# Two key tiles, then two value tiles: reordering the loads of a decode attention kernel group by group

## The chip, the core and the metric

The kernel runs on one core of a Trainium2 chip. The metric is the device time of one execution in microseconds (us), median of the runs shown. All tiles are float32.

## What is computed

The program adds three things for a batch of two rows: the input `x`, a sliding-window attention over a key and a value cache, and a gated feed-forward layer. Both branches take the same normalised `x`.

```python
xn = _layernorm(x)                                   # x: [2, 1, 512]
q = xn @ wq                                          # 32 heads of 128
k = k_cache[:, :, Sk - W:, :]                        # 8 kv heads, W = 4096 rows of 128, each kv head for 4 q heads
v = v_cache[:, :, Sk - W:, :]
p = softmax(q . k * 128 ** -0.5)
A = (p . v) @ wo                                     # wo: [4096, 512]
gate, up = xn @ W_gate, xn @ W_up                    # [512, 1792] each
h = gate * (gate > 0) * up
B = h @ W_down                                       # [1792, 512]
return x + A + B
```

## The kernel before

**Loads.** Everything large comes through one ring of four buffers of 4 MB (tag `ring`, pool at L62), on SyncE's queue (`load`, L71 to L74): 23 loads in the order in which the code calls them. A load waits, on that queue and in order, until the buffer of the load four places ahead of it has been used up. The order is: wq in two tiles (L122), `wg` and `wu` (L226, L227), then in the loop at L395 one tile of keys and one tile of values in turn, then `wd` (L413) and `wo` in two tiles, the second in four pieces (L449 to L452). `x` comes on ScalarE's queue in five pieces (L119 to L121); the tile `x2` is read by the layer norm (L188, L203) and, at the end, by the residual (L419 to L422).

**Front.** The layer norm, the transposed `xn` (L211), `q` (L221), the layout of `q` in `qz` (L248) and the gate and up products (L258) with their gating (L263 to L276) stand ahead of the attention.

**Attention.** There are four groups g (two batch rows, two halves of the kv heads), and each has two tiles a = 0, 1 of keys and of values, a tile holding 4096 rows of two heads. `scores(g, a)` (L288) turns a key tile with four VectorE transposes of 128x2048 (L298), two for each half s1 into its own buffer `kT` (pool `ktp` has two, so the next tile's transposes wait until TensorE has read the buffer), and then issues the score matmuls (L308) into one tile `s`. Between the two halves it runs what stands in the list `late`. After a = 1 come `maxima` (L313: row maximum on VectorE, two small matmuls, `nm`), `softmax` (L334: one ScalarE exponential), and `turn` (L340: two matmuls `pp`, a VectorE transpose to `pt`, and the sums' reciprocal). `values(g, a)` (L351) multiplies `pt` with a value tile into `o`. `gather(g, a)` (L364) masks `o` on VectorE (`on`, L367) and folds it with a matmul (`oa`, L373); `finish(g)` (L377) adds up and divides (`su`, `osb`); `spread_heads(r)` (L385) lays out two finished groups for `wo`.

**Order.** The schedule is manual (L68): each engine gets its instructions in the order of the code. In the loop at L395 the values of group g-1 stand behind the scores of group g:

```python
kt_in = load_kv(k_cache, "k", g, a)
v_in = load_kv(v_cache, "v", g - 1, a) if g else None
scores(g, a, kt_in)
if a:
    turn(g, *softmax(g, maxima(g)))
if g:
    values(g - 1, a, v_in)
    late.append(lambda g=g, a=a: gather(g - 1, a))
```

So `values(g-1, 0)` runs on TensorE while VectorE turns the second key tile of group g, and `values(g-1, 1)` while it turns the first of group g+1. The values of group 3 follow behind the loop (L442 to L445), then the down product, `spread_heads(1)` and the `wo` products into `y4` and `y_ps` (L431, L438), a copy and the store (L463, L464).

Of the kernel before, what the change touches and what calls it, by code (L numbers as in the profile page):

```python
# [9 lines left out]
F32 = mybir.dt.float32  # L10
# [10 lines left out]
def kernel(  # L21
# [12 lines left out]
    nc = tc.nc  # L34
    P = 128
    B, _, D = x.shape
# [12 lines left out]
    NG = B * R  # L49
# [5 lines left out]
    NP = C // 2  # L55
# [5 lines left out]
    const = ctx.enter_context(tc.tile_pool(name="const", bufs=1))  # L61
# [9 lines left out]
    def load(name, src, shape):  # L71
        t = ring.tile(shape, F32, name=name, tag="ring")
        nc.sync.dma_start(t, src)
        return t  # L74


    def load_wq(m):
        src = wq[m * 2 * P:(m + 1) * 2 * P, :].rearrange("(p k) f -> p k f", p=P)
        return load(f"wq{m}", src, [P, 2, HQ * DH])
# [20 lines left out]
    def load_kv(cache, name, g, a):  # L100
        r, b = divmod(g, B)
        base = cache[b, r * C + a, SK - W:SK, :]
        run = J * DH
        src = bass.AP(
            tensor=cache.tensor, offset=base.offset, ap=[[run, PK], [NP * SK * DH, 2], [1, run]]
        )
        return load(f"{name}{g}_{a}", src, [P, run])
# [9 lines left out]


    x2 = const.tile([B, D], F32, name="x2")  # L119
    for c0, c1 in ((0, 256), (256, 320), (320, 384), (384, 448), (448, 512)):  # L120
        nc.scalar.dma_start(x2[:, c0:c1], x[:, 0, c0:c1])  # L121
    wqt = [load_wq(m) for m in range(2)]  # L122

    ident = const.tile([P, P], F32, name="ident")
# [83 lines left out]
    for kc in range(KC):  # L208
        m, k = divmod(kc, 2)
# [7 lines left out]
    for kc in range(KC):  # L217
        for r in range(R):
            for c in range(C):
# [3 lines left out]
                    start=(kc == 0), stop=(kc == KC - 1),  # L223
# [31 lines left out]
    for h, dst, wt in ((0, g_ps, gw), (1, u_ps, uw)):  # L255
        for kc in range(KC):
            for c in range(Q):
                nc.tensor.matmul(  # L258
                    dst[32 * c:32 * c + 32, :], xnT[:, 1, kc, :], wt[:, kc, c * MQ:(c + 1) * MQ],
                    start=(kc == 0), stop=(kc == KC - 1),  # L260
# [25 lines left out]
    late = []  # L286

    def scores(g, a, kt_in):  # L288
        if a == 0:
            ss[g] = ps_s.tile([P, 512], F32, name=f"s{g}", tag="s")  # L290
        kts = []
        for s1 in range(S1):
            kt = ktp.tile([P, JH, CB, KL, 2], F32, name=f"kT{g}_{a}_{s1}", tag="kT")
            kts.append(kt)
            for n in range(2):
                lo = JH // 2 * n
                j = JH * s1 + lo
                nc.vector.transpose(  # L298
                    kt[:, lo:lo + JH // 2].rearrange("p j c k h -> p (j c k h)"),
                    kt_in[:, j * DH:(j + JH // 2) * DH],  # L300
                )
            while late:
                late.pop(0)()
        for cb in range(CB):
            for s1 in range(S1):
                for h in range(2):
                    lo = 32 * (2 * s1 + h)
                    nc.tensor.matmul(  # L308
                        ss[g][lo:lo + 32, :], qz[:, g, cb, h, 16 * a:16 * a + 32], kts[s1][:, :, cb, :, h],
                        start=(a == 0 and cb == 0), stop=(a == NP - 1 and cb == CB - 1),  # L310
                    )

    def maxima(g):  # L313

        m = work.tile([P, 1], F32, name=f"m{g}", tag="m")
        nc.vector.tensor_reduce(out=m, in_=ss[g], op=ALU.max, axis=AX.X)  # L316
        mt = ps_1.tile([1, P], F32, name=f"mt{g}", tag="misc")
        nc.tensor.transpose(mt, m, ident)
        mx = work.tile([1, C, REP], F32, name=f"mx{g}", tag="mx")
        nc.vector.tensor_reduce(  # L320
            out=mx, in_=mt.rearrange("p (s x b i) -> p x i s b", s=S1, x=C, b=PB), op=ALU.max, axis=AX.XY
        )
        mb = work.tile([1, S1, C, PB, REP], F32, name=f"mb{g}", tag="mb")
        for s1 in range(S1):
            nc.vector.tensor_scalar(
                mb[:, s1], mx[:, :, None, :].to_broadcast([1, C, PB, REP]), -SCALE, None, op0=ALU.mult
            )
        nm_ps = ps_1.tile([P, 1], F32, name=f"nm_ps{g}", tag="misc")
        nc.tensor.matmul(nm_ps, mb.rearrange("p s x b i -> p (s x b i)"), ones, start=True, stop=True)
        nm = work.tile([P, 1], F32, name=f"nm{g}", tag="nm")  # L330
        nc.vector.tensor_copy(nm, nm_ps)  # L331
        return nm

    def softmax(g, nm):  # L334
        p = work.tile([P, 512], F32, name=f"p{g}", tag="p", bufs=1)
        l = work.tile([P, 1], F32, name=f"l{g}", tag="l")
        nc.scalar.activation(p, ss[g], AF.Exp, bias=nm, scale=SCALE, accum_out=l)  # L337
        return p, l

    def turn(g, p, l):  # L340
        pp = ps_kt.tile([P, 2, 512], F32, name=f"pp{g}", tag="kt")
        for h in range(2):
            nc.tensor.matmul(pp[:, h], perm[:, h], p, start=True, stop=True)  # L343
        pts[g] = work.tile([P, NP * S1, JH, HK], F32, name=f"pt{g}", tag="pt")
        nc.vector.transpose(pts[g].rearrange("p n j k -> p j n k"), pp.rearrange("p h y -> p y h"))  # L345
        lp = ps_1.tile([HR, 1], F32, name=f"lp{g}", tag="misc")
        nc.tensor.matmul(lp, by_h.rearrange("p x i -> p (x i)"), l, start=True, stop=True)
        rls[g] = work.tile([HR, 1], F32, name=f"rl{g}", tag="rl")
        nc.vector.reciprocal(rls[g], lp)

    def values(g, a, v):  # L351
        o = ps_1.tile([P, 512], F32, name=f"o{g}_{a}", tag="o")
        for s1 in range(S1):
            for jh in range(2):
                for q in range(Q):
                    j = 16 * jh + 4 * q
                    lo = (JH * s1 + j) * DH
                    nc.tensor.matmul(  # L358
                        o[32 * q:32 * q + 32, :], pts[g][:, a * S1 + s1, j:j + 4, :].rearrange("p u k -> p (u k)"), v[:, lo:lo + 512],
                        start=(s1 == 0 and jh == 0), stop=(s1 == S1 - 1 and jh == 1),  # L360
                    )
        os[a] = o

    def gather(g, a):  # L364

        ons[a] = work.tile([P, 4, P], F32, name=f"on{g}_{a}", tag="on")
        nc.vector.tensor_tensor(  # L367
            ons[a], os[a].rearrange("p (u d) -> p u d", u=4), mask[:, :, None].to_broadcast([P, 4, P]), op=ALU.mult
        )

        if a == 0:
            oa[g] = ps_1.tile([HR, 4, P], F32, name=f"oa{g}", tag="oa")
        nc.tensor.matmul(  # L373
            oa[g], picks[:, a].rearrange("p h a i -> p (h a i)"), ons[a], start=(a == 0), stop=(a == NP - 1)
        )

    def finish(g):  # L377
        r, b = divmod(g, B)
        if b == 0:
            osb[r] = const.tile([HR, B, P], F32, name=f"osb{r}")  # L380
        su = work.tile([HR, P], F32, name=f"su{g}", tag="su", bufs=1)
        nc.vector.tensor_reduce(out=su, in_=oa[g].rearrange("h u d -> h d u"), op=ALU.add, axis=AX.X)  # L382
        nc.vector.tensor_scalar(osb[r][:, b], su, rls[g], None, op0=ALU.mult)

    def spread_heads(r):  # L385
        op = ps_1.tile([P, NJ, B], F32, name=f"op{r}", tag="misc")
        for e in range(NE):
            nc.tensor.matmul(  # L388
                op, spread[:, e].rearrange("h k e -> h (k e)"),
                osb[r][:, :, e * NJ:(e + 1) * NJ].rearrange("h b j -> h j b"),  # L390
                start=(e == 0), stop=(e == NE - 1),
            )
        nc.vector.tensor_copy(oT[:, r, :, :, 0], op)

    for g in range(NG):  # L395
        for a in range(NP):
            kt_in = load_kv(k_cache, "k", g, a)
            v_in = load_kv(v_cache, "v", g - 1, a) if g else None
            scores(g, a, kt_in)
            if a:  # L400
                turn(g, *softmax(g, maxima(g)))
            if g:
                values(g - 1, a, v_in)
                late.append(lambda g=g, a=a: gather(g - 1, a))
                if a:
                    late.append(lambda g=g: finish(g - 1))
                elif g % B == 1 and g > 1:
                    late.append(lambda g=g: spread_heads((g - 2) // B))
    while late:
        late.pop(0)()  # L410
    g = NG - 1
    vin = [load_kv(v_cache, "v", g, a) for a in range(NP)]
    dw = load_down()  # L413


# [2 lines left out]
    for e in range(Q):  # L418
        nc.tensor.matmul(  # L419
            y_ps[32 * e:32 * e + 17, :], xsel.rearrange("p b s -> p (b s)")[:, 0:17],  # L420
            x2[:, e * P:(e + 1) * P], start=True, stop=False,
        )  # L422

    y4 = ps_kt.tile([P, D], F32, name="y4", tag="kt")
# [14 lines left out]
                y_ps[32 * e:32 * e + 17, :], lhsT, w[:, e * P:(e + 1) * P], start=False, stop=stop  # L439
            )  # L440

    for a in range(NP):  # L442
        values(g, a, vin[a])
        gather(g, a)
    finish(g)  # L445
    for k in range(FM):
        slot(hT[:, k], dw[:, k])
    spread_heads(R - 1)
# [44 lines left out]
```

## Time and profile before

| | us |
|---|---|
| median of 3 runs | 236.75 (236.08 to 237.97) |
| the profiled execution | 236.89 |
| its span in the trace | 235.1 |
| PE busy | 145.4 (62%) |
| DVE busy | 102.5 (44%) |
| ACT busy | 8.3 (4%) |

PE is TensorE's matmul side, PEld its weight load, DVE VectorE, ACT ScalarE, POOL GpSimd, SPq SyncE's queue. Times in the trace are counted from the start of the span. The chain of waits starts at the last instruction and goes back, at each step, to what released it; a row gives start, length and what ran. A row of the timeline adds, in brackets, how long the engine had been idle before and what ended that. A row of the waits gives the total, the number of times and the longest. "x22" at a matmul counts records: a float32 matmul of 128x512 leaves two.

### The profile page before, as it was taken

What the parts mean: (1) busy time and instruction counts of PE and PEld (TensorE: products, weight loads), DVE (VectorE), ACT (ScalarE), POOL (GpSimd) and SP (SyncE); (2) the same over time, 40 slices, a digit from 0 to 9 for tenths busy, and PEclk for the clock granted to TensorE, in tenths of its full rate; (3) what the DMA queues carried; (4) which work ended last, traced back from release to release, by engine and by line L of the source; (5) the groups of instructions that cost most, each with busy time, mean ns of one, the idle gap of its engine ahead of it and who ended that gap; (6) DMA issues with size and microseconds to landing.
All of it is one profiled execution on the core that took longest, in us unless ns stands there. A gap on an engine that the chain in (4) does not pass through costs nothing.

```text
span 235.1 us, 2205 instructions
## 1 busy us (share of the span) xinstructions
PE 145.4 (62%) x948; PEld 48.0 (20%) x948; DVE 102.5 (44%) x121; ACT 8.3 (4%) x27; POOL 8.1 (3%) x31
## 2 busy tenths in 40 slices
PE   0009964953634743685596295677388485877993
PEld 0006234220100110121221030121022212212433
DVE  2040012249377249397248759209827712322101
ACT  0001021300000010000100000010000001000000
POOL 8400000000000000000000000000000000000000
PEclk9999995785596895599859889958979978899999
DMA  7999999999999999899999999999999999989950
GB/s 268 446 446 424 415 444 418 438 446 440 413 421 420 440 440 440 362 429 424 435 393 413 379 429 438 440 440 390 446 440 427 446 429 414 426 376 410 410 212 1
DMA packets 3784, 95.03 MB, mean 404 GB/s; under 512 B 438, under 2 KB 448, under 8 KB 704
## 3 DMA queue, kind: packets, MB, share of 16 engines
q1 hardware_dynamic: 3756, 94.90, 95.1%
q8 instruction: 7, 0.11, 0.2%
q14 instruction: 1, 0.01, 0.0%
q10 hardware_dynamic: 20, 0.00, 0.0%
HBM read 94.90 MB, written 0.00 MB: 404 GB/s over the span
## 4 chain that ended last, share of the span: by engine, by line
PE 47%; DVE 40%; issue 6%; POOL 3%; ACT 2%; POOLq 0%; ACTq 0%; DVEq 0%
DVE kT L298 29%; PE s L308 15%; PE pp L343 5%; PE o L358 5%; PE q_ps L221 4%; PE y L431 4%; PE oa L373 3%; DVE on L367 2%; PE g_ps L258 2%; PE op L388 2%; DVE pt L345 2%; PE xt_ps L211 2%; PE u_ps L258 1%; ACT p L337 1%; PE rq L239 1%
## 5 line engine op out<-in xcount | busy, mean ns | idle before, releaser
L298 DVE STREAM_TRANSPOSE kT<-k 128x2048 f32<-128x2048 f32 x32 | 71.5, 2278 | 18.3 <-PE s L308 18.3
L308 PE MATMUL s<-kT,qz 128*32 128x512 f32 x256 | 53.1, 786 | 41.1 <-DVE kT L298 41.1
L358 PE MATMUL o<-v,pt 128*32 128x512 f32 x256 | 35.6, 647 | 0.0
L308 PEld LDWEIGHTS s<-kT,qz 128*32 128x32 f32 x256 | 11.0, 135 | 76.4 <-DVE kT L298 51.1
L343 PE MATMUL pp<-p,perm 128*128 128x512 f32 x16 | 12.2, 906 | 4.7 <-ACT p L337 4.7
L211 PE MATMUL xt_ps<-rep,xn 2*128 2x32 f32 x16 | 3.7, 400 | 17.5 <-DVE xn L205 17.5
L358 PEld LDWEIGHTS o<-v,pt 128*32 128x32 f32 x256 | 10.6, 119 | 18.6 <-issue 18.6
L373 PE MATMUL oa<-on,picks 128*16 128x512 f32 x16 | 8.3, 598 | 8.4 <-DVE on L367 8.4
L345 DVE STREAM_TRANSPOSE pt<-pp 128x1024 f32<-128x1024 f32 x4 | 5.0, 1250 | 16.1 <-PE pp L343 16.1
L316 DVE TENSOR_REDUCE m<-s 128x1 f32<-128x512 f32 x4 | 2.8, 691 | 18.7 <-PE s L308 18.7
L367 DVE TENSOR_TENSOR on<-o,mask 128x512 f32<-128x512 f32 x8 | 5.3, 664 | 12.0 <-PE o L358 12.0
L221 PE MATMUL q_ps<-wq,xnT 128*32 128x512 f32 x64 | 10.0, 792 | 0.5 <-DVE xnT L213 0.5
L337 ACT ACTIVATE p<-s,nm 128x512 f32<-128x512 f32 x4 | 2.7, 687 | 147.2 <-DVE nm L331 147.2
L211 PEld LDWEIGHTS xt_ps<-rep,xn 2*128 2x128 f32 x16 | 3.6, 320 | 17.5 <-issue 17.5
L248 DVE COPY qz<-rq 32x32 f32<-32x32 f32 x16 | 3.0, 187 | 7.1 <-ACT qz L248 7.1
L188 DVE BATCH_NORM_STATS2 stats<-x 2x6 f32<-2x512 f32 x1 | 0.7, 682 | 11.7 <-DMA x<-in_A_x_dram 11.7
L236 DVE COPY qT<-qt 128x32 f32<-128x32 f32 x2 | 0.4, 191 | 11.9 <-PE qt L232 11.9
L431 PE MATMUL y<-wo,oT 128*32 128x512 f32 x48 | 5.4, 594 | 0.0
L343 PEld LDWEIGHTS pp<-p,perm 128*128 128x128 f32 x16 | 3.7, 256 | 8.0 <-issue 4.2
L258 PE MATMUL g_ps<-wg,xnT 128*32 128x448 f32 x32 | 4.9, 772 | 0.0
L382 DVE TENSOR_REDUCE su<-oa 16x128 f32<-16x512 f32 x4 | 2.7, 679 | 4.5 <-PE oa L373 4.5
L431 PE MATMUL y<-wd,hT 128*32 128x512 f32 x28 | 4.5, 595 | 0.0
(79 smaller groups left out, 67.0 us busy)
## 6 DMA issues: line engine op xcount, KB each, us to landing
k<-in_A_k_cache_dram SPq DMA_DIRECT2D x8, 4096.0 KB, 21.7
v<-in_A_v_cache_dram SPq DMA_DIRECT2D x8, 4096.0 KB, 21.3
wq<-in_A_wq_dram SPq DMA_DIRECT2D x2, 4096.0 KB, 17.0
wo<-in_A_wo_dram SPq DMA_DIRECT2D x1, 4096.0 KB
wg<-in_B_W_gate_dram SPq DMA_DIRECT2D x1, 3584.0 KB
wu<-in_B_W_up_dram SPq DMA_DIRECT2D x1, 3584.0 KB
wd<-in_B_W_down_dram SPq DMA_DIRECT2D x1, 3584.0 KB, 20.6
wo<-in_A_wo_dram SPq DMA_DIRECT2D x1, 2048.0 KB
```

The costliest lines, as they stand in the source:

```text
L211: nc.tensor.matmul(xt_ps[:, o, kc, :], cols, rep.rearrange("r s b -> r (s b)"), start=True, stop=True)
L221: nc.tensor.matmul(q_ps[r][32 * c:32 * c + 32, :], xnT[:, 0, kc, :], wqt[kc // 2][:, kc % 2, n * 512:(n + 1) * 512], start=(kc == 0), stop ...
L258: nc.tensor.matmul(dst[32 * c:32 * c + 32, :], xnT[:, 1, kc, :], wt[:, kc, c * MQ:(c + 1) * MQ], start=(kc == 0), stop=(kc == KC - 1),)
L298: nc.vector.transpose(kt[:, lo:lo + JH // 2].rearrange("p j c k h -> p (j c k h)"), kt_in[:, j * DH:(j + JH // 2) * DH],)
L308: nc.tensor.matmul(ss[g][lo:lo + 32, :], qz[:, g, cb, h, 16 * a:16 * a + 32], kts[s1][:, :, cb, :, h], start=(a == 0 and cb == 0), stop=(a ...
L337: nc.scalar.activation(p, ss[g], AF.Exp, bias=nm, scale=SCALE, accum_out=l)
L343: nc.tensor.matmul(pp[:, h], perm[:, h], p, start=True, stop=True)
L345: nc.vector.transpose(pts[g].rearrange("p n j k -> p j n k"), pp.rearrange("p h y -> p y h"))
L358: nc.tensor.matmul(o[32 * q:32 * q + 32, :], pts[g][:, a * S1 + s1, j:j + 4, :].rearrange("p u k -> p (u k)"), v[:, lo:lo + 512], start=(s ...
L367: nc.vector.tensor_tensor(ons[a], os[a].rearrange("p (u d) -> p u d", u=4), mask[:, :, None].to_broadcast([P, 4, P]), op=ALU.mult)
L373: nc.tensor.matmul(oa[g], picks[:, a].rearrange("p h a i -> p (h a i)"), ons[a], start=(a == 0), stop=(a == NP - 1))
L431: nc.tensor.matmul(y4[32 * t:32 * t + 32, :], lhsT.rearrange("p b s -> p (b s)"), w, start=(i < Q), stop=(i >= EARLY - Q))
```

## The change

The loop of a group now loads its two key tiles and its two value tiles together, in this order, computes both halves of the scores and the softmax, and then multiplies its own values, `gather(g, 0)` standing between `values(g, 0)` and `values(g, 1)`. Only `gather(g, 1)`, `finish(g)` and, for g = 1, `spread_heads(0)` go into `late`, which the first key tile of the next group runs between its halves. The block behind the loop that did the values of group 3 falls away. The layer norm's `x2` comes in three pieces, not five; a second copy `xr` of `x` in two pieces, behind them on the same queue, feeds the residual.

```diff
-    for c0, c1 in ((0, 256), (256, 320), (320, 384), (384, 448), (448, 512)):
+    for c0, c1 in ((0, 256), (256, 384), (384, 512)):
         nc.scalar.dma_start(x2[:, c0:c1], x[:, 0, c0:c1])
+    xr = const.tile([B, D], F32, name="xr")
+    for c0 in (0, D // 2):
+        nc.scalar.dma_start(xr[:, c0:c0 + D // 2], x[:, 0, c0:c0 + D // 2])
...
     for g in range(NG):
+        kt_in = [load_kv(k_cache, "k", g, a) for a in range(NP)]
+        v_in = [load_kv(v_cache, "v", g, a) for a in range(NP)]
         for a in range(NP):
-            kt_in = load_kv(k_cache, "k", g, a)
-            v_in = load_kv(v_cache, "v", g - 1, a) if g else None
-            scores(g, a, kt_in)
-            if a:
-                turn(g, *softmax(g, maxima(g)))
-            if g:
-                values(g - 1, a, v_in)
-                late.append(lambda g=g, a=a: gather(g - 1, a))
...
+            scores(g, a, kt_in[a])
+        turn(g, *softmax(g, maxima(g)))
+        for a in range(NP):
+            values(g, a, v_in[a])
+            if a + 1 < NP:
+                gather(g, a)
+        late.append(lambda g=g: (gather(g, NP - 1), finish(g)))
+        if g % B == 1 and g + 1 < NG:
+            late.append(lambda g=g: spread_heads(g // B))
...
-            x2[:, e * P:(e + 1) * P], start=True, stop=False,
+            xr[:, e * P:(e + 1) * P], start=True, stop=False,
...
-    for a in range(NP):
-        values(g, a, vin[a])
-        gather(g, a)
-    finish(g)
+    while late:
+        late.pop(0)()
```

More of the change, by code (lines that the diff above doesn't have):

```diff
@@ L395 @@
     for g in range(NG):
+        kt_in = [load_kv(k_cache, "k", g, a) for a in range(NP)]
+        v_in = [load_kv(v_cache, "v", g, a) for a in range(NP)]
         for a in range(NP):
-            kt_in = load_kv(k_cache, "k", g, a)
-            v_in = load_kv(v_cache, "v", g - 1, a) if g else None
-            scores(g, a, kt_in)
-            if a:
-                turn(g, *softmax(g, maxima(g)))
-            if g:
-                values(g - 1, a, v_in)
-                late.append(lambda g=g, a=a: gather(g - 1, a))
[L405 to L412, printed above, removed]
+            scores(g, a, kt_in[a])
[7 more added lines that the diff above has]
+            late.append(lambda g=g: spread_heads(g // B))
     dw = load_down()
```

## The prediction

> **What bounds the kernel now.** I read the page first, then the waits, then the chain of waits, then the loads. The page has the transfer engines busy in nearly every slice, so the first question is whether the loads or the computation set the end.
>
> ```profile
> span 235.1 us, 2205 instructions
> ...
> DMA  7999999999999999899999999999999999989950
> ```
>
> The waits answer it: they name who stood still and for whom (total, times, longest).
>
> ```profile
> DVE kT L298 <- PE s L308: 18.3, 4, 4.9
> ...
> DVE pt L345 <- PE pp L343: 16.1, 4, 4.7
> ...
> DVE on L367 <- PE o L358: 12.0, 3, 4.6
> DVE stats L188 <- DMA x<-in_A_x_dram: 11.7, 1, 11.7
> ```
>
> The last row is the only one in which a computing engine waits for loaded data, once, at the start. No transpose ever waits for its keys and no matmul for its values. So VectorE and TensorE hand the work to each other, and the transfers are busy because four ring buffers let them keep pace. The chain shows the hand-over for group 2:
>
> ```profile
> 122.14 4.40 DVE kT L298 x2
> 126.54 0.59 DVE on L367
> ...
> 133.69 4.34 PE s L308 x22
> 138.06 4.51 DVE kT L298 x2
> ...
> 147.60 3.82 PE s L308 x21
> 151.44 0.70 DVE m L316
> ...
> 154.78 3.79 PE pp L343 x4
> 158.59 1.25 DVE pt L345
> 159.88 4.40 DVE kT L298 x2
> ```
>
> The reader should see one group as three stages: key tile 0 until its buffer is free again, 122.14 to 138.06, 15.92 us; key tile 1 until the scores are complete, to 151.44, 13.38 us; the softmax until `pt` is there, 158.59 + 1.25 = 159.84, 8.40 us. A group costs 159.88 - 122.14 = 37.74 us. No value matmul is on the chain in it: they run on TensorE while VectorE transposes.
>
> **The change part by part.** *The group's own values.* VectorE's queue now has `on(g, 0)`, which needs all of `values(g, 0)`, ahead of the next group's transposes. `values(g, 0)` needs `pt`, the last step of the softmax. So the value matmuls of one tile, and the mask, leave the shelter of the transposes and stand alone on the chain, once a group. Behind the waiting `on` in VectorE's queue stand all transposes of the next group, and behind these TensorE's scores. Their prices are in the tail of this run, which already has this order, and the last softmax is there as well:
>
> ```profile
> 181.95 1.91 PE op L388 x16
> ...
> 184.10 4.40 DVE kT L298 x2
> ...
> 193.74 0.70 DVE m L316
> ...
> 199.89 4.46 PE o L358 x29
> 204.37 0.70 DVE on L367
> ...
> 207.82 3.62 PE o L358 x32
> 211.46 0.70 DVE on L367
> ...
> 229.97 2.20 PE y_ps L438 x72
> ```
>
> ```profile
> 199.81 1.25 DVE L345 STREAM_TRANSPOSE pt<-pp 128x1024 f32<-128x1024 f32 x1 [3.66 <-PE pp L343]
> ```
>
> One value tile costs 211.46 - 207.82 = 3.64 us, or 204.37 - 199.89 = 4.48 us in the other row. I take 3.64: as at 207.82, TensorE has worked shortly before. With the mask (0.70) and two short hand-overs of some 0.05 us each it is 4.4 us a group. `values(g, 1)` stays covered: behind `on(g, 0)` come `oa` and 32 matmuls (3.6 us) while VectorE makes the first two transposes (4.40). It ends some 5 us after them started, so `on(g, 1)`, which stands behind these transposes in VectorE's queue, waits about 0.4 us; without cover it would cost 3.6.
>
> *Tile 0.* In the middle it keeps what group 2 had there before (`on`, `oa`, `su`, `osb`), so it keeps its row, 15.92 us, plus the 0.4. In group 0 nothing is in the middle. `spread_heads(0)` moves from the middle of group 3's second tile to the middle of group 2's first: 184.10 - 181.95 = 2.15 us on the chain in both places, no gain.
>
> *Tile 1.* Before, TensorE did the older group's values during these transposes; now it has nothing. Group 0 of this run had no values either, and is the row for it:
>
> ```profile
> 52.12 8.90 DVE kT L298 x4
> ...
> 61.07 4.81 PE s L308 x24
> ...
> 74.84 5.61 PE s L308 x28
> 80.48 0.70 DVE m L316
> ...
> 83.78 1.97 PE pp L343 x4
> 85.77 1.25 DVE pt L345
> ```
>
> ```profile
> 65.90 8.89 DVE L298 STREAM_TRANSPOSE kT<-k 128x2048 f32<-128x2048 f32 x4 [4.89 <-PE s L308]
> ```
>
> Tile 0 of group 0 takes 65.90 - 52.12 = 13.78 us, tile 1 takes 80.48 - 65.90 = 14.58 us, against 13.38 in group 2, although group 2 has a mask in it. The difference is TensorE after idling: 28 records in 5.61 us against 21 in 3.82 behind busier stretches. Removing the interleaved values therefore makes the scores dearer as well. I take 14.58 for every group; the other end is 13.38 - 0.6 = 12.8.
>
> *Softmax.* Rows: 87.02 - 80.48 = 6.54 us in group 0, 8.40 in group 2, 199.81 + 1.25 - 193.74 = 7.32 in group 3. The difference is `pp`, 1.97 or 3.79 us, and with it the granted clock (the column before the last two):
>
> ```profile
> 84.00:88.00 4.00, 1.86 (x6) 0.54 (x5) 2.23 (x3) 0.00 (x0) 0.00 (x0) 1.00 1.09 467
> ```
>
> ```profile
> 155.00:160.00 5.00, 5.00 (x14) 1.40 (x18) 1.41 (x3) 0.00 (x0) 0.00 (x0) 0.50 1.00 433
> ```
>
> TensorE's gap ahead of `pp` is the same in both, from 74.84 + 5.61 to 83.78 and from 147.60 + 3.82 to 154.78, 3.3 us, so it doesn't decide alone. What TensorE did before resembles group 0, but one row is little; I take the middle, 7.3, ends 6.54 and 8.40. [...]
>
> *x in three pieces.* The five pieces delay the layer norm by 11.7 us. The trace doesn't say what one piece costs; the gain lies between 0 and, whatever x does, what the first keys allow:
>
> ```profile
> 28.27 18.42 SPq L73 DMA_DIRECT2D k<-in_A_k_cache_dram  x3
> ```
>
> ```profile
> k<-in_A_k_cache_dram SPq DMA_DIRECT2D x1, 4096.0 KB, 22.4
> ```
>
> The first key tile lands at 28.27 + 22.4 = 50.67, and transposing starts at 52.12. So at most 1.45 us come through, unless the transfers, full from the start, get faster. I take all of it, since two pieces of five, in equal shares of the 11.7, are 4.7 us, more than the keys allow; the ends are 50.7 and 52.12. The loads of `xr` stand behind x2's on ScalarE's queue, whose first work comes after the layer norm: nothing.
>
> *Order of the loads.* The same bytes in the same ring. The key tile of group 1 moves from third to fifth place behind the first one.
>
> ```profile
> 74.82 0.54 SPq L73 DMA_DIRECT2D v<-in_A_v_cache_dram  x1
> ```
>
> ```profile
> v<-in_A_v_cache_dram SPq DMA_DIRECT2D x1, 4096.0 KB, 24.7
> ```
>
> This load is the sixth of the cache (first: 50.67) and lands at 99.52, so a load takes (99.52 - 50.67) / 5 = 9.77 us, and the fifth lands at 89.75. VectorE wants it at 90.7 (below), so there is 1 us to spare; a later landing would be paid in full. After that a group computes for 42.7 us and loads for 4 x 9.77 = 39.1, so the loads get ahead and wait for buffers. SyncE's queue keeps its order, since buffers come free in it: keys, keys, values, values. The last tile of `wo` waits for `values(3, 0)` to end, near 220:
>
> ```profile
> 204.36 9.67 SPq L452 DMA_DIRECT2D wo<-in_A_wo_dram  x5
> ```
>
> ```profile
> wo<-in_A_wo_dram SPq DMA_DIRECT2D x1, 256.0 KB, 15.1
> ```
>
> Its last piece took 15.1 us to land with other loads ahead of it, so it is there by 235.2. It is needed where the y_ps matmuls start, 235.1 - 229.97 = 5.1 us before the end, at 238.6: covered.
>
> *The sum.* Group 0: 50.7 + 13.78 + 14.58 + 7.3 + 4.4 = 90.76. Group 1: 15.92 + 0.4 + 14.58 + 7.3 + 4.4 = 42.6, to 133.4. Group 2: 42.6 + 2.15 = 44.75, to 178.1. Group 3 up to the start of `on(3, 0)`: 42.6 - 0.7 = 41.9, to 220.0. From that mask on (211.46 before) the order is as before: 235.1 - 211.46 = 23.64. Span 243.7. The profiled execution took 236.89 for a span of 235.1, 1.8 more, so 245.5; the median is 0.14 under it: **245.3 us**, 3.6% slower. In short: each of the later groups is nearly 5 us longer and group 0 about 5.5, some 20 us by the end of the loop, and about half of it comes back, because `values(2, 1)`, `finish(2)` and `values(3, 0)` no longer stand as a block behind the loop.
>
> **Rivals.**
> *The loads set the end, and the order is nearly free.* For it: the row of nines. Against it: no transpose or matmul waits for data. The point that decides: at the last group the transposes would wait for keys. The last piece of `wo` lands at about 213.5 + 15.1 = 228.6 in any order (its issue is the end of the row at 204.36, 204.36 + 9.67 = 214.0, less one issue of about 0.5), and 6.5 us later the span ends: 235.1, so 236.8. [...]
> *Full clock in every softmax.* 7.3 becomes 6.54 four times, 3.0 us less: 242.3. For: group 0. Against: groups 2 and 3. [...]
> *Half clock in softmax and values.* 8.40 for 7.3 and 4.48 for 3.64 in four groups, 7.8 us more: 253. For: TensorE is busy less evenly than before. Against: a `pp` at half clock is itself 3.8 us of work ahead of the values.
> *VectorE runs ahead.* If the next group's transposes were queued ahead of `on(g, 0)`, the 4.4 us would be hidden in groups 0 to 2, 13.2 less, but the loads would then hold the end: about 235. Against: the manual order, and VectorE's waits at `pt` (16.1) with the next keys already there.
>
> **How the numbers follow.** Forecast 0.60; full clock 0.15; half clock 0.15; loads set the end 0.06; VectorE ahead 0.02; anything else that ends faster 0.02. About 1% is what a measurement can tell from no change. Within 1% are the loads and VectorE ahead, 0.08; faster 0.02; slower 0.90. The low end, 240.5, takes in the full clock and the cheaper tile 1 in one or two groups; the high end, 251, takes x without a gain (1.4) and half of the half-clock case (3.9). Outside lie the 0.10 on the other side and part of the half clock.
>
> **What would show it.** Right: in the chain, from group 0 on, `pt`, o, `on`, kT in a row, o with about 3.6 us and `on` waiting for it in all four groups; the start of tile 0 in groups 1 to 3 about 42 to 45 apart; tile 1's scores at 28 or so records in 5 to 6 us; the share of the transfers falling behind 100 us, and SPq waiting longer for buffers. First transposes near 50.7, waiting for keys. Wrong: transposes waiting for keys in later groups (loads), o off the chain (VectorE ahead), `pp` near 2 us everywhere (242), or o over 4.5 everywhere (253).

## The result and the profile after

The changed kernel takes 252.66 us (median of 6 runs, 249.66 to 256.57) against 237.42 (6 runs): ratio 1.058, 95% interval 1.052 to 1.065. It is slower, as forecast, but by more: the forecast was 245.3 and the range ended at 251. The profiled execution has a span of 250.0 us; 243.7 was predicted. The medians take in every execution, but this ratio and all those below leave out executions more than 1.5% above the fastest of their kernel, three of the changed kernel's six, and the second profile of the changed kernel, further down, is of such an execution.

Lines of the changed file stand 3 lower than before (L298 is now L301, L358 L361, L367 L370). First the page's row of the transfer engines and two rows of the waits:

```profile
DMA  7999999999999999999999999999169999946900
```

```profile
DVE on L370 <- PE o L361: 26.5, 8, 6.0
...
DVE kT L301 <- DMA k<-in_A_k_cache_dram: 2.4, 1, 2.4
```

The mask waited for value matmuls 3 times before, 12.0 us in all; now 8 times, 26.5. One transpose waits for keys, the first. The transfers have a hole from 175 us on: the loads are ahead and wait for buffers, the next value tile being issued at 182.03, when the older one has been used. Then the chain:

```profile
50.55 8.90 DVE kT L301 x4
...
84.94 1.25 DVE pt L348
...
86.25 3.69 PE o L361 x32
89.96 0.70 DVE on L370
...
106.88 0.04 DVE kT L301
...
115.82 5.40 PE s L311 x26
121.25 0.70 DVE m L319
...
124.52 2.42 PE pp L346 x4
126.96 1.25 DVE pt L348
...
128.26 5.91 PE o L361 x32
134.19 0.70 DVE on L370
...
142.35 3.05 PE op L391 x16
...
176.15 5.86 PE o L361 x32
182.03 0.70 DVE on L370
...
220.53 5.86 PE o L361 x32
226.41 0.70 DVE on L370
```

The order of the steps is the predicted one: `pt`, then o, then the mask, in all four groups. The sizes are not. The masks start at 89.96, 134.19, 182.03 and 226.41; the prediction's sum puts them at 90.06, 132.7, 177.4 and 220.0. Group 0 is right to 0.1 us, and each later group is 1.6 to 3.1 us too long. The row to read is o: 3.69 us in group 0, 5.91, 5.86 and 5.86 in the others, the same 32 records. The windows over these matmuls say why. A row gives the window and its length, then busy time and records of PE, PEld, DVE, ACT and POOL, and last the granted clock, the transfers' share and their GB/s:

```profile
86.00:90.00 4.00, 3.64 (x32) 0.94 (x32) 0.27 (x3) 0.00 (x0) 0.00 (x0) 1.00 1.05 451
...
129.00:132.00 3.00, 3.00 (x20) 0.79 (x16) 0.00 (x0) 0.00 (x0) 0.00 (x0) 0.50 0.96 415
...
176.00:179.00 3.00, 2.85 (x16) 0.79 (x20) 0.13 (x2) 0.00 (x0) 0.00 (x0) 0.50 0.00 0
```

Group 0 has its values at full clock (1.00), groups 1 and 2 mostly at half (0.50, and 0.82 from 132 us, 0.74 from 179). In the last window nothing is being loaded at all (share 0.00), so traffic is not what slows these matmuls. The stretch between the scores and `pp`, in which TensorE has two small matmuls only, is 3.3 us in groups 0 and 1 alike (79.65 to 82.95 and 121.25 to 124.52), with a granted clock of 1.00 in both, so it alone doesn't decide either.

### The profile page after: what moved, and what is told of

It is laid out like the page before. It is cut to its first block, busy times and chain, and to the rows that moved or that the text cites. A ratio compares the mean times of both kernels' runs of the same rounds, so it can differ in the third digit from the quotient of the medians.

```text
span 250.0 us, 2211 instructions
## 1 busy us (share of the span) xinstructions
PE 153.1 (61%) x948; PEld 49.2 (20%) x948; DVE 103.0 (41%) x121; ACT 8.3 (3%) x27; POOL 8.1 (3%) x31
## 4 chain that ended last, share of the span: by engine, by line
PE 49%; DVE 28%; DMA 10%; issue 7%; POOL 3%; ACT 1%; POOLq 0%; ACTq 0%; DVEq 0%
DVE kT L301 19%; PE s L311 16%; PE o L361 14%; DMA k<-in_A_k_cache_dram 10%; PE pp L346 4%; PE y L429 4%; PE oa L376 3%; PE q_ps L224 3%; DVE on L370 2%; DVE pt L348 2%; PE op L391 2%; PE xt_ps L214 1%; ACT p L340 1%; DVE m L319 1%; PE y_ps L436 1%
## 5 line engine op out<-in xcount | busy, mean ns | idle before, releaser
L311 PE MATMUL s<-kT,qz 128*32 128x512 f32 x256 | 56.8, 865 | 49.6 <-DVE kT L301 49.6
L301 DVE STREAM_TRANSPOSE kT<-k 128x2048 f32<-128x2048 f32 x32 | 71.4, 2281 | 21.1 <-PE s L311 18.8
L361 PE MATMUL o<-v,pt 128*32 128x512 f32 x256 | 38.5, 708 | 4.8 <-DVE rl L352 4.8
L370 DVE TENSOR_TENSOR on<-o,mask 128x512 f32<-128x512 f32 x8 | 5.5, 692 | 26.5 <-PE o L361 26.5
L361 PEld LDWEIGHTS o<-v,pt 128*32 128x32 f32 x256 | 10.6, 128 | 25.8 <-issue 20.6
L214 PE MATMUL xt_ps<-rep,xn 2*128 2x32 f32 x16 | 3.7, 400 | 13.8 <-DVE xn L208 13.8
L346 PE MATMUL pp<-p,perm 128*128 128x512 f32 x16 | 9.3, 707 | 4.7 <-ACT p L340 4.7
L214 PEld LDWEIGHTS xt_ps<-rep,xn 2*128 2x128 f32 x16 | 3.6, 320 | 13.8 <-issue 13.8
L391 PE MATMUL op<-osb,spread 16*128 16x32 f32 x32 | 5.0, 314 | 1.1 <-DVE osb L386 1.1
L391 PEld LDWEIGHTS op<-osb,spread 16*128 16x128 f32 x32 | 4.8, 231 | 2.8 <-DVE osb L386 2.0
```

Source lines behind the costliest of these rows:

```text
L214: nc.tensor.matmul(xt_ps[:, o, kc, :], cols, rep.rearrange("r s b -> r (s b)"), start=True, stop=True)
L301: nc.vector.transpose(kt[:, lo:lo + JH // 2].rearrange("p j c k h -> p (j c k h)"), kt_in[:, j * DH:(j + JH // 2) * DH],)
L311: nc.tensor.matmul(ss[g][lo:lo + 32, :], qz[:, g, cb, h, 16 * a:16 * a + 32], kts[s1][:, :, cb, :, h], start=(a == 0 and cb == 0), stop=(a ...
L361: nc.tensor.matmul(o[32 * q:32 * q + 32, :], pts[g][:, a * S1 + s1, j:j + 4, :].rearrange("p u k -> p (u k)"), v[:, lo:lo + 512], start=(s ...
L370: nc.vector.tensor_tensor(ons[a], os[a].rearrange("p (u d) -> p u d", u=4), mask[:, :, None].to_broadcast([P, 4, P]), op=ALU.mult)
L391: nc.tensor.matmul(op, spread[:, e].rearrange("h k e -> h (k e)"), osb[r][:, :, e * NJ:(e + 1) * NJ].rearrange("h b j -> h j b"), start=(e ...
```

## The experiments

Theories at this point: the values, now alone on the chain, are the loss, and TensorE's clock, 0.50 over most of the values in groups 1 and 2, makes it larger, as an effect of the idle stretches that the new order leaves (chain and clock); against it, that the order of the loads is the loss, or that the values are slow for another reason than the clock.

**x alone.** The kernel before with the two edits on x, in five rounds.

```diff
-    for c0, c1 in ((0, 256), (256, 320), (320, 384), (384, 448), (448, 512)):
+    for c0, c1 in ((0, 256), (256, 384), (384, 512)):
...
+    xr = const.tile([B, D], F32, name="xr")
```

> The kernel before with x in three pieces and the second copy for the residual; loads and order of the groups untouched. Chain theory (TensorE and VectorE hand the work to each other, loads are early): the first transposes start when the first keys land, near 50.6 us, not at 52.1, and the whole chain moves with them: about 1.5 us less, ratio 0.994. Loads theory (the last tile of wo sets the end): its landing doesn't move, so the time doesn't either, ratio 1.00.

Ratio 1.0004 (0.996 to 1.005). The timeline shows the start as expected, waiting for keys:

```profile
50.81 8.89 DVE L301 STREAM_TRANSPOSE kT<-k 128x2048 f32<-128x2048 f32 x4 [2.63 <-DMA k<-in_A_k_cache_dram]
```

Of the 1.3 us won there against 52.12, 0.6 is left in this execution's span (234.5 against 235.1), less than the runs of either kernel differ among themselves. The interval takes in both nothing and 0.4%, but not the 0.6% that the chain theory gave. The x edits move the start and can't be seen in the time.

**Order of the loads alone.** Both key tiles of a group, then both value tiles, with the computation as before, so that each value tile waits in the ring for the next group's scores.

```diff
     for g in range(NG):
+        kt_in = [load_kv(k_cache, "k", g, a) for a in range(NP)]
...
-            scores(g, a, kt_in)
+            scores(g, a, kt_in[a])
...
-                values(g - 1, a, v_in)
+                values(g - 1, a, v_in[a])
+                v_next.append(load_kv(v_cache, "v", g, a))
```

> The kernel before (values one group behind) with the loads of the change's order: both key tiles of a group, then both value tiles. Theory (the order of the loads has to be that in which buffers come free): the loads of group g's values wait for the older values to be used, and the next keys stand behind them in the queue, so the keys of groups 2 and 3 come some 25 us late each: 280 to 300 us. Rival (a ring of four takes any order): 236 to 240 us.

One execution, 256.02 us, against 236.6 for the kernel before. The direction is that of the theory, the size is not: 25 us a group was far too much.

```profile
DVE kT L298 <- DMA k<-in_A_k_cache_dram: 14.5, 3, 7.9
```

Keys come late three times, 14.5 us in all, of the 19 us that the execution is longer; where the rest goes was not followed up. So this order of loads is no good without the order of the computation that goes with it. In the changed kernel, where both moved, keys are late only at the start, by 2.4 us: the loads are not its loss.

**The values covered again.** The change's loads and its own softmax, but `gather(g, 0)` and `values(g, 1)` go into the middle of the next group's first key tile, and `gather(g, 1)` with `finish(g)` into its second.

```diff
+    def second(g, v):
+        gather(g, 0)
+        values(g, 1, v)
...
-        for a in range(NP):
-            values(g, a, v_in[a])
-            if a + 1 < NP:
-                gather(g, a)
-        late.append(lambda g=g: (gather(g, NP - 1), finish(g)))
+        values(g, 0, v0)
+        late.append(lambda g=g, v1=v1: second(g, v1))
```

> The changed kernel with its loads and its own values straight behind the softmax, but gather(g, 0) and values(g, 1) moved into the middle of the next group's first key tile, and gather(g, 1) with finish(g) into the middle of its second. So the next group's first two transposes cover values(g, 0). Theory 1 (the exposed values(g, 0) and its mask are the loss, 5.9 + 0.7 us a group): 6.6 us less at groups 1 and 2, about 1 at group 0, where the keys land at 89.5, perhaps 1 back per group for the later scores: 237 to 241 us, ratio to before 1.00 to 1.015. Theory 2 (the dearer second key tile and the new load order are the loss, the values are hidden enough): 248 us or more, ratio 1.045 or more.

Median 244.17 us, ratio 1.032 (1.024 to 1.040), between the two. From the chain and the waits of this run:

```profile
116.78 5.99 PE s L311 x28
...
131.19 5.65 PE o L361 x32
136.86 0.70 DVE on L370
...
174.47 4.40 DVE kT L301 x2
178.87 0.59 DVE on L370
```

```profile
DVE kT L301 <- DMA k<-in_A_k_cache_dram: 7.3, 2, 4.2
```

In group 2 (174.47) the transposes cover the values wholly, and the mask follows without a wait; in group 1 o takes 5.65 us and sticks out beyond two transposes. What is left has other places: the second tile's scores still take 5.99 us, and with a shorter group 0 the keys of group 1 are late by 4.2 us, since they now stand fifth. Covering the values takes away about half of the loss (3.2% is left of 5.8%, and of the 14.9 us in the spans 7.8 are gone).

**The clock.** Three kernels are the changed one with matmuls of constants, called fillers here, in gaps of TensorE. Nobody reads their result, a tile that takes turns with `o` in one buffer; they only add work.

```diff
+    def warm(n):
+        t = ps_1.tile([P, 512], F32, name="warm", tag="o")
+        for i in range(n):
+            lo = 32 * (i % Q)
+            nc.tensor.matmul(t[lo:lo + 32, :], fold, spot.rearrange("p c b e -> p (c b e)"), start=True, stop=True)
...
+        warm(2)
         mt = ps_1.tile([1, P], F32, name=f"mt{g}", tag="misc")
...
+        warm(2)
         nm_ps = ps_1.tile([P, 1], F32, name=f"nm_ps{g}", tag="misc")
...
+        warm(4)
         pp = ps_kt.tile([P, 2, 512], F32, name=f"pp{g}", tag="kt")
...
+        warm(4)
         rls[g] = work.tile([HR, 1], F32, name=f"rl{g}", tag="rl")
```

These are the gaps of the softmax stage:

> As the run with all fillers, but without the 28 ahead of the second key tile's scores: only the gaps of the softmax stage are filled. Clock theory: o 3.7 us in every group and softmax near 6.5, tile 1 still near 14.4: about 9 us less than the changed kernel, 242 to 244 us, ratio 1.025. Rival (another reason): o stays near 5.9, 250 to 254 us.

Median 246.66 us, ratio 1.046 (1.040 to 1.053); the profiled span is 245.0. The chain in group 1:

```profile
115.92 5.57 PE s L311 x25
...
125.48 1.98 PE pp L355 x4
...
128.86 3.67 PE o L371 x32
```

o is 3.67 and `pp` 1.98 us, in this group and, to 0.03 us, in all others, with the same value tiles, weights and loads; the granted clock over these matmuls is 1.00 in all four groups. These are the lengths of group 0 in the changed kernel, 3.69 and 1.97, at a granted clock of 1.00. The scores ahead still take 5.57 us. So the clock is the reason for the 5.9. The gain is 5 us in the span and not 9, since tile 0 and tile 1 of groups 1 and 3 came out slower here than in the first profile, by some 1.0 and 0.7 us.

The next adds 28 matmuls ahead of the second key tile's scores:

```diff
         for a in range(NP):
+            if a:
+                warm(28)
             scores(g, a, kt_in[a])
```

> The changed kernel with matmuls of constants, whose results nobody reads, in TensorE's gaps: 28 ahead of the second key tile's scores, 2 ahead of each of the two small matmuls of the maxima, 4 ahead of pp and 4 behind the sums. It only adds work. Clock theory (values(g, 0) takes 5.9 us instead of 3.6, and the second tile's scores are slow, because TensorE has idled and is at half clock): o 3.7 us in every group, tile 1 near 13 us, softmax near 6.5; 238 to 241 us, ratio near 1.01. Rival (the value matmuls are slow for another reason, such as the loads' traffic or the weights): o stays near 5.9 us, and the time stays at 250 to 254 us, ratio 1.055 or more.

Median 243.41 us, ratio 1.028 (1.019 to 1.036): a smaller gain than expected, for a reason that the windows of group 1 show.

```profile
114.00:116.00 2.00, 0.09 (x4) 0.09 (x8) 1.85 (x1) 0.00 (x0) 0.00 (x0) 1.00 1.14 492
116.00:118.00 2.00, 2.00 (x16) 0.54 (x20) 0.00 (x0) 0.00 (x0) 0.00 (x0) 0.74 0.92 393
118.00:120.00 2.00, 2.00 (x12) 0.44 (x8) 0.00 (x0) 0.00 (x0) 0.00 (x0) 0.50 0.99 426
```

The fillers end some 2 us before the transposes do. That one gap, with TensorE busy before and after it, is followed by half clock (0.74, then 0.50), in the midst of the scores, which take 4.9 us. The same happens in group 2, behind a gap of 2.06 us. In groups 0 and 3 the gap is 1.64 and 1.76 us, the clock stays at 1.00 and the scores take 2.9 and 3.25 us, so there the 28 did their work. The last kernel fills this gap too, with 38, and puts 22 ahead of the first tile's scores:

```diff
-                warm(28)
+                warm(38)
...
+        if a == 0:
+            warm(22)
         for cb in range(CB):
```

> The changed kernel with all the fillers of the earlier run, 38 instead of 28 ahead of the second key tile's scores (the 28 ended 2 us early), and 22 ahead of the first tile's scores. Clock theory: at full clock in all stages a group costs 38 to 39 us (tile 0 15, tile 1 12.7, softmax 6.5, values and mask 4.4); the span ends near 231 by the chain, near 234 if the loads bind: 233 to 237 us, ratio 0.985 to 1.005, so the whole loss of the change is TensorE's clock. Rival (the exposed values and masks cost by themselves what they cost, the clock is a part only): 240 us or more, ratio 1.015 or more.

Median 237.59 us, ratio 1.004 (1.001 to 1.008); span 235.2. The page's row of the clock (tenths of full speed, 40 slices), the chain of group 1 with two later masks, and the wait for keys:

```profile
PEclk9999976997699999999999979999999999999999
```

```profile
113.31 3.53 PE s L319 x26
...
124.33 3.67 PE o L373 x32
...
172.28 0.70 DVE on L382
...
211.53 0.70 DVE on L382
```

```profile
DVE kT L307 <- DMA k<-in_A_k_cache_dram: 4.9, 2, 3.4
```

The scores of tile 1 go from 5.40 to 3.53 us, o from 5.91 to 3.67, the last mask from 226.41 to 211.53, which is where it stood in the kernel before (211.46). Filling TensorE's gaps takes 14.8 us out of the changed kernel's span, about all that the change had put in (14.9). Two waits for keys are left: 3.4 us at the start and 1.5 for the keys of group 1, which stand fifth and are now wanted sooner. The number is that of the clock theory, just above its range in us and within it as a ratio; that the exposed values cost nothing doesn't follow yet, since the kernel before has idle gaps too. The last two runs close this.

**The changed kernel once more.**

> The changed kernel once more, unchanged. [...] Rival (a fixed reason in groups 1 to 3): o 3.7 in group 0 and 5.9 in groups 1, 2 and 3 again.

It took 255.95 us in the profiled execution and 248.93 in another. Its chain (span 254.2 us; o of the four groups, `pp` of groups 0, 2 and 3):

```profile
83.31 3.77 PE pp L346 x4
...
88.40 5.61 PE o L361 x32
...
132.20 5.89 PE o L361 x32
...
176.17 2.00 PE pp L346 x4
...
179.50 3.69 PE o L361 x32
...
219.73 3.79 PE pp L346 x4
...
224.85 5.66 PE o L361 x32
```

Now group 0 has the slow values and group 2 the quick ones, in the same program. It isn't a property of a group; what decides in one execution where the clock is low stays open. It also fits the wide spread of this kernel's first six runs, 6.9 us against 1.9 before: the longer the run, the lower its mean granted clock, from 0.821 at 249.66 us to 0.786 at 256.57. That the clock makes all of the spread was not shown.

**The kernel before, with fillers.** The fillers of the last kernel, without the 38 and without the 4 behind the sums, in the kernel before with the edits on x.

```diff
+        if a == 0:
+            warm(22)
...
+        warm(4)
         pp = ps_kt.tile([P, 2, 512], F32, name=f"pp{g}", tag="kt")
```

> The kernel before with x as in the change and with matmuls of constants in TensorE's gaps: 22 in the first key tile's stage, 2 ahead of each of the two small matmuls of the maxima, 4 ahead of pp. Clock theory: pp 2 us in all groups instead of 3.8 and the first tile's scores nearer 3 us than 4.4, some 7 to 9 us less on the chain; but the loads, which are full throughout, let the last piece of wo land no earlier than near 228, so the span ends at 233 to 234: 234.5 to 236 us, ratio 0.99 to 1.0. If the loads' landing doesn't bind, 228 to 231 us, ratio 0.97.

Median 235.02 us, ratio 0.994 (0.990 to 0.997); span 233.8. Within the expectation, but not for its reason: the loads don't hold the end there, the chain simply lost less than 7 us. Two rows of it, group 3:

```profile
188.43 4.95 PE s L319 x25
...
197.45 1.99 PE pp L357 x4
```

`pp` has its short length (1.97 us at a granted clock of 1.00 in the kernel before), the second tile's scores ahead of it don't (4.95 us for 25 records, where group 1 of the last kernel took 3.53 for 26). So the next version also fills that stage, behind the older group's values, and group 0, which has none:

```diff
-        if a == 0:
-            warm(22)
+        warm(22 if a == 0 else 12 if g else 38)
```

> The filled kernel before, with more fillers: also 12 ahead of the second key tile's scores, behind the older group's values, and 38 there in group 0, which has no values. Clock theory: the scores of the second tile, 4.5 to 5 us in groups 1 and 3 of the first filled version, come down to 3.4 to 3.8, so 2 to 4 us leave the chain; the last piece of wo lands near 227 us and the y_ps matmuls can't start ahead of it, so 232 to 234 us, ratio 0.98 to 0.99. If the fillers end too early or too late to help: 235 us, ratio 0.994, as in the first version.

Median 231.66 us, ratio 0.980 (0.976 to 0.985), span 229.9: faster than both kernels, and a little below the 232 to 234 expected. Rows of its chain, of SyncE's timeline, of the loads and of the waits:

```profile
184.25 3.82 PE s L318 x30
...
200.71 5.31 PE o L371 x32
...
226.56 0.46 PE y_ps L451 x8
```

```profile
197.25 10.55 SPq L465 DMA_DIRECT2D wo<-in_A_wo_dram  x5
```

```profile
wo<-in_A_wo_dram SPq DMA_DIRECT2D x1, 256.0 KB, 19.2
```

```profile
PEld y_ps L451 <- DMA wo<-in_A_wo_dram: 0.3, 1, 0.3
```

The last piece of `wo` is issued about 0.5 us before 207.8 and lands 19.2 us later, near 226.5; the last y_ps matmuls start at 226.56. TensorE's weight loads wait 0.3 us for it: here, as in no other kernel of this study, the chain and the loads end together. The row at 200.71 is a surprise. It is the place of the row at 207.82 in the kernel before, behind the same two gaps of 0.83 and 1.27 us, where o took 3.62 us; here the granted clock goes from 1.00 before 200 us to 0.50 between 202 and 204, and o takes 5.31.

With both orders filled the account of the change can be drawn up, roughly. By the profiled spans, filling takes 235.1 - 229.9 = 5.2 us out of the kernel before (the edits on x included) and 14.8 out of the changed one; what is left between the two filled ones is 235.2 - 229.9 = 5.3. By the ratios, each against the kernel before in the same session, a loss of 5.8% becomes one of 2.4% (1.004 against 0.980), some 5.6 of 13.8 us. So of the 14 to 15 us about 5 to 6 are the order itself, values and masks on the chain in spite of the shorter end and the 1.5 us of waiting for group 1's keys, and about 8 to 10 are clock that the new order loses beyond what the old one lost. The split can't be made sharper. The filled kernel before isn't at full clock throughout (mean 0.926 against 0.964 in the other, and the row at 200.71), which makes the order's share come out too small; some fillers of the other run over their gap, by 1.9 us in group 2's first tile (its transposes end at 142.80, the fillers at 144.68), which makes it too large.

## Why the prediction was wrong

**Right: what bounds the kernel.** A chain of TensorE and VectorE, not the loads. "The loads set the end" (0.06) would have left 236.8.

**Right: the start.** First transposes at 50.55 us, waiting for keys, for 50.7 predicted. In the kernel before, these edits alone brought nothing measurable. That group 0 comes out to 0.1 us is luck: its softmax takes 6.54 us (79.65 to 86.19) for 7.3, its two tiles 14.27 and 14.83 for 13.78 and 14.58.

**Right: the order of the loads.** The keys of group 1 are in time by a hair: they are wanted at 90.66 us, and kernels that ask for them sooner get them at 89.74 (values covered) and 89.86 (every gap filled), for 89.75 predicted. The last tile of `wo` is covered; the end from the last mask on is 250.0 - 226.41 = 23.6 us, as predicted. The loads get ahead later than forecast: the transfers' share was to fall behind 100 us and stays in the nines up to 175.

**Wrong: the price of the values.** The step that failed is "I take 3.64: as at 207.82, TensorE has worked shortly before". It measured 5.91, 5.86 and 5.86 us in three groups, 6.7 us over, more than the whole miss of 6.3 in the span. The row at 207.82 comes from the end of the kernel, where TensorE has been at work since 197.07 with gaps of 0.83 and 1.27 us. In the loop the values stand behind a stage in which it mostly waits. The fillers showed it: with the softmax stage filled and nothing else changed o is 3.67 in every group. The kernel before had rows of the right place, value tiles straight behind the softmax, hidden under transposes (its timeline of TensorE, groups 1 and 2):

```profile
120.81 4.73 PE L358 MATMUL o<-v,pt 128*32 128x512 f32 x29
...
158.56 4.63 PE L358 MATMUL o<-v,pt 128*32 128x512 f32 x29
```

With the 4.48 at 199.89 these are all the value tiles straight behind the softmax, and none comes near 3.64, the row at a granted clock of 1.00. They would still have been too low: at 120.81 the granted clock is 0.50 up to 123 us, some 2 us into the tile, in the new order at 128.26 up to 132, nearly 4 us into it.

**Wrong: the half-clock rival.** It had 0.15, a price of 4.48 for o, from a row that is half slow and half quick (granted clock 0.59 up to 202 us, 1.00 behind it), and an argument against it that doesn't hold: "a `pp` at half clock is itself 3.8 us of work ahead of the values". In the second profile `pp` takes 3.77 us and o behind it 5.61. An estimate from above would have been twice the quick row, 7.3 us, since the lowest granted clock in the traces of both kernels, in windows of 1 us, is 0.50 and a `pp` at 0.50 took 3.79 us for 1.97 at 1.00; the range with it goes well beyond 251. The rival's 253 us lies near the measured 252.66, but by errors of opposite sign: it has every softmax at 8.40, where 6.54 to 7.08 was measured, and o at 4.48, where it was 5.86 to 5.91 in three groups.

**Mis-sized, smaller.** `spread_heads(0)`, "no gain", costs 1.1 us more: its matmuls take 3.05 us for 1.91. The softmax, taken at 7.3, measures 128.21 - 121.25 = 7.0 in group 1, where its `pp` is part full, part half clock (1.00 up to 125.5 us, 0.50 from 126.2). Tile 1, taken at 14.58 from group 0, measures 14.4 there (106.88, its start in the same chain, to 121.25). The "about 5.5" for group 0 in the prediction's short form is 5.2 by its own rows, 40.06 against 87.02 - 52.12 = 34.90; the sum doesn't use it.

## What to carry to other kernels

Work that moves out of another engine's shelter is to be priced at the clock it will have in the new place: from rows of the like place, not from the quickest one. One such row is not enough, since the same place gave 3.69 and 5.91 us within one execution; twice the full-clock time is an estimate from above, by the lowest granted clock seen here, 0.50. The new order here gathers TensorE's work and with it its idle time, and by the rough split above that cost one and a half to two times as much as the exposed work. Matmuls that compute nothing are a cheap test for it, and left in, with the edits on x, they made the kernel before about 2% faster.

## What was not expected of the hardware

A gap of about 2 us between two busy stretches of TensorE was followed by a clock of 0.50 (2.08 us ahead of 115.91 in the kernel with 28 fillers), while gaps of 1.64 and 1.76 us in the same execution were not. No length of gap follows from this: in the filled kernel before, two gaps of 0.83 and 1.27 us ahead of the values at 200.71 were followed by 0.50; in the kernel before the same two ahead of the values at 207.82 were not. With all gaps filled the mean granted clock rose from 0.816 to 0.964 and the changed kernel got 15 us quicker (252.66 to 237.59) while the count of its matmul records rose from 948 to 1524. And one program's slow groups moved from one execution to the next: o took 3.69 us in group 0 and 5.86 in group 2, then 5.61 and 3.69.
